# Decay attention with two gated layers on one core: weights converted by 32-bit passes, states summed on TensorE, idle products taken out, orders made anew

## Chip, core and metric

One core of a Trainium2 chip runs the whole program in one launch. The metric is the device time of an execution in microseconds. The kernel before took 938.72 us, the median of three runs (938.11 to 939.4).

## What is computed

An attention with a decaying state, then two dense layers with gates, in float32 and with float64 weights that come as they are (q, k, v, alpha: 4 batches, 8 heads, 768 positions, 48 columns; weights 384 x 2048 and 2048 x 384 for each layer):

```python
for t in range(S):
    state = alpha[:, :, t, :, None] * state + np.einsum('bhd,bhe->bhde', k[:, :, t], v[:, :, t])
    y[:, :, t] = np.einsum('bhd,bhde->bhe', q[:, :, t], state)
x = y as rows of 384 columns                  # 3072 rows
h = x @ w_in;  x = (h * np.tanh(softplus(h))) @ w_out     # first layer
h = x @ w_in2; return (h * np.cos(h)) @ w_out2            # second layer
```

## The kernel before

**Attention in pieces.** The positions are cut into 12 steps `u` of 64; each step has two pieces `(u, hb)`, 24 in all, each for half of the batches and all heads. A piece loads alpha, k, q and v, takes two running products along the positions on DVE (`scan`, L316, and `scan2`, L334), scales k and q by them (`keys`, L338, and `queries`, L348, on DVE or POOL by the sets `KPOOL` and `QPOOL`), transposes k on PE (`turn`, L366), multiplies keys and queries (`scores`, L380 and L381), masks them out of PSUM (`causal`, L388 to L391) and multiplies by v and by the state at once (`out_mm`, L401 to L405): rows of the left tiles `VE`, `VO` (`three`) hold v and the state, rows of the right tiles `RE`, `RO` the scores and the queries. Both pieces of a step share one pair `RE0`, `RO0`.

**States.** After a piece's output, `state_mm` (L465) makes the step's own product, `state_add` (L477) adds it to the state in `VE` and `VO` by four DVE instructions that read PSUM (L475: four copies on ACT in the first step), and `state_mul` (L485) scales it by the step's decay by two instructions on POOL or, for the numbers in `MULS`, on DVE. The next step's output needs it.

**Weights.** For each of 16 slices of a layer, `load_w` (L220) brings 768 float64 columns as pairs of 32-bit words, and six passes make a float32 of each, split into a rounded part `wh` and a rest `wl`: `conv_x` takes bits of the low word or of 16 bits of the high one (L230, L232 or L235), `conv_s` the sign (L241 or L244), `conv_b` scales (L251 or L253), `conv_c` merges (L257), `conv_d` rounds (L261 or L263) and `conv_e` subtracts (L267). Strings and sets at the head (`TOPS`, `SIGNS`, `SCALES`, `ROUNDS`, `LOWS`) choose engine and form: `v` with a 16-bit result on DVE, `b` a 32-bit shift on DVE, `a` ACT, `p` POOL and so on. The raw words of the second layer use the two `three` tiles in turn.

**Layers.** A step of 512 rows and one slice is `mm1` (nine products, L528 to L530), the gate on ACT and DVE, a split of the gate's result (`act_c`, L567 or L569, and `pool_c`, L574, on DVE or POOL) and `mm2` (nine products into three sums, L589 to L591). The first six slices of the first block are done in halves of 256 rows, two slices at a time. There are 192 `mm1` and 192 `mm2`.

**Order.** `Plan` takes all these pieces with an engine, an assumed cost, a due time and what they wait for, and plays them through: on each engine the piece that is ready and due first goes next. What comes out is written down in that order, and the engines follow it with semaphores. Due times come from the numbers at the head (`START`, `EARLY`, `CONV` and so on). Up to 40 idle products (`idle`, L517, 112x128 of a constant) fill PE's wait until the first `mm2`; 28 are issued. `last_heads` (L410), `fill` (L416), `y_hi` (L424) and `y_lo` (L430) hand the first four steps' outputs to the first layer.

Of the kernel before, what the change touches and what calls it, by code (L numbers as in the profile page):

```python
# [25 lines left out]
P = 128  # L26
# [10 lines left out]
START = [1448.3, 429.36, -76.954, 70.35, -175.51, -140.25, 526.61, -216.63, -872.8, 815.57]  # L37
ATT = 92.272
T0 = 526.27
HALVES = {(0, 0): 6}  # L40
SHARED = {(0, 0): 8, (0, 4): 9, (1, 0): 10}
EARLY = [-310.76, -66.363, -294.04, -73.698, 257.15, 404.09, 543.88, 902.74]
BASE = [-469.62, -69.328, 128.04, 9.9207]
BESIDE = [0, 2, 8, 7]
LAG = 0.27
LOAD_K = -68.961
LOAD_Q = -195.56
LOAD_V = 275.37
LOAD_W = 205.5
LATE = -166.65  # L50
SPLIT = [-29.4, 68.92]
CONV = [-1263, -1320.3, 881.42, 1950, -719.73, -157.26, -760.27, -551.95, -520.44, -19.586, -1457.4, -895.42, 142.68, 1400, 785.88, 1646.4, -310.36, -245.74, -228.26, -324.75, 1573, -1266, -775.74, 735.74, -740.32, 1124.8, -569.28, -195.03, -1333.7, -55.12, -2911.9, -506.3]
ELEM = 226.61
SECOND = -472.6
EVAC = -278.38
FILLED = 162.76
AHEAD = (0, 0, 0, 0, 0, 14, 6, 5, 27, 12, 27, 8, 24, 8, 12, 19)
FILL = 4
QPOOL = {*range(0, 2), *range(3, 9), 12, *range(15, 18), 20, *range(22, 24)}
MULS = {*range(7, 9), *range(10, 13), 14, *range(16, 19), 21}  # L60
LOWS = {*((0, fc) for fc in (2, 3, 10, 14, 15,)), *((1, fc) for fc in (1, 6, 10, 11, 13, 15,))}
GLS = {*range(0, 3), 5, *range(7, 9), 10, 12, *range(16, 18), *range(19, 21), 23, *range(26, 29), *range(30, 33), 34, *range(38, 40), 43, *range(45, 47), 48, *range(50, 54), *range(55, 57), *range(61, 63), *range(64, 66), 69, 71, 73, *range(76, 82), *range(86, 88), *range(89, 91), *range(92, 95), *range(97, 99), *range(100, 105), *range(108, 112), 113, *range(115, 117), *range(119, 122), 126, 129, 132, 134, 136, *range(138, 142), 145, 155, *range(157, 159), 161, 163, 167, 170, 174, 178, 180, *range(184, 186), *range(187, 189), *range(190, 192), *range(193, 199)}
IDLE = 40
KPOOL = {0, 2, 5, 7, *range(9, 11), *range(12, 18), 23}
# [3 lines left out]
ROUNDS = {*((0, fc) for fc in (0, 3, 6, 8, 9, 10, 11, 12, 13, 14,)), *((1, fc) for fc in (0, 2, 3, 4, 5, 7, 10, 11, 14, 15,))}  # L68
# [3 lines left out]
CASTS = {0, *range(2, 4), 7, *range(10, 13), *range(18, 21), *range(22, 25), 26, *range(28, 31), *range(32, 35), 36, 38, *range(42, 45), *range(47, 49), 50, 52, *range(54, 56), 57, 59, 62, 69, 73, *range(86, 88), *range(90, 92), 93, 96, 98, 102, 105, 108, *range(110, 113), *range(116, 120), 121, *range(123, 125), *range(126, 132), 133, *range(135, 137), *range(138, 140), *range(141, 143), 148, *range(150, 153), *range(154, 157), 161, *range(163, 165), 168, *range(172, 174), 175, *range(179, 181), 182, *range(185, 189), 190, *range(192, 194), 195, 197, 199}  # L72
# [9 lines left out]
class Plan:  # L82


    def __init__(self, bufs):
        self.bufs, self.pieces, self.names = bufs, [], {}
# [6 lines left out]
    def order(self):  # L93
        n = len(self.pieces)
        waits, users = [0] * n, [[] for _ in range(n)]
        holds, taken = {}, {}
        for i, (name, _, _, _, _, after, takes, drops) in enumerate(self.pieces):
            for a in after:
                if a in self.names:
                    waits[i] += 1  # L100
                    users[self.names[a]].append(i)
# [4 lines left out]
        events, out = [], []  # L106

# [12 lines left out]
        while len(out) < n:  # L120
            for e, q in ready.items():
                if free[e] > now:
                    continue
                for j, (_, i) in enumerate(q):
                    name, _, cost, _, run, _, takes, _ = self.pieces[i]
                    if may_take(takes):
                        del q[j]
                        for tag, tile_ in takes:
                            taken.setdefault(tag, []).append(tile_)
                        cost, lag = cost(now) if callable(cost) else (cost, LAG)  # L130
                        free[e] = now + cost
                        heapq.heappush(events, (now + cost, -1, i))
                        heapq.heappush(events, (now + cost + lag, 1, i))
                        out.append(run)
                        break
            if len(out) == n:
                break
# [5 lines left out]
            for tile_ in self.pieces[i][7]:  # L143
# [5 lines left out]
            for u in users[i]:  # L149
# [7 lines left out]
def chunked_path(ctx: ExitStack, tc: tile.TileContext, q, k, alpha, v1, ve, vo, w1, w2, const, out):  # L157
# [16 lines left out]
    seg_start = sb.tile([112, W65], F32, name="seg_start")  # L174
    nc.vector.memset(seg_start, 0.0)
# [164 lines left out]
    def queries(s, eng):  # L340
# [5 lines left out]
        if s not in R_:  # L346
            R_[s] = RE0, RO0
# [685 lines left out]
```

## Time and profile before

| | |
|---|---|
| median of three runs | 938.72 us |
| profiled execution, its own time | 937.42 us |
| span of the profiled execution | 935.6 us |
| PE busy | 910.2 us, 97% |
| VectorE (DVE), ScalarE (ACT), GpSimd (POOL) busy | 618.1, 668.1, 341.6 us |
| mean granted TensorE clock | 0.987 |

The span goes from the first to the last instruction. A float32 attention product counts as two instructions on PE. PE's busy time takes in the latency of overlapping products, so the count of products in a stretch says more about its pace than the share. On DVE and POOL, an instruction's duration holds what it waited for inside the engine.

### The profile page before, as it was taken

The numbers are of one execution on the slowest core, as the hardware profiler recorded it, in microseconds if no ns is written. First come the engines' busy times: TensorE is split into PE (matmuls) and PEld (weight loads), VectorE is DVE, ScalarE is ACT, GpSimd is POOL, SyncE is SP. The second block draws the span as 40 slices with busy tenths as digits, with TensorE's granted clock in tenths as the row PEclk, the third lists the DMA queues.
The fourth block names the chain that finished last, engine by engine and source line by source line (L and its number), as shares of the span: only waits on it lengthen the run. The fifth ranks groups of instructions, "written<-read, shape, count | busy, mean of one in ns | idle before, by whom it ended". The sixth has DMA issues, their size and how long they took to land.

```text
span 935.6 us, 15419 instructions
## 1 busy us (share of the span) xinstructions
PE 910.2 (97%) x6046; PEld 743.6 (79%) x6046; DVE 618.1 (66%) x876; ACT 668.1 (71%) x1030; POOL 341.6 (37%) x242
## 2 busy tenths in 40 slices
PE   8889999999999999999998999999999999999997
PEld 6678877788887787788887778888888888888886
DVE  7998999947756858733498889874545434444442
ACT  3569798989878888799998855756645555554553
POOL 4666437132235213432248443323413134122211
PEclk9689999999999999999999999999999999999999
DMA  8554334113113213120023013200000000000000
GB/s 235 168 175 129 135 121 136 55 35 96 58 59 88 83 35 104 51 73 1 1 102 101 1 68 115 89 1 1 34 35 1 0 34 1 35 1 0 35 1 36
DMA packets 25181, 59.08 MB, mean 63 GB/s; under 512 B 3856, under 2 KB 7568, under 8 KB 25104
## 3 DMA queue, kind: packets, MB, share of 16 engines
q1 hardware_dynamic: 25104, 58.05, 19.2%
q8 instruction: 48, 0.79, 0.3%
q14 instruction: 29, 0.24, 0.1%
HBM read 52.53 MB, written 4.72 MB: 61 GB/s over the span
## 4 chain that ended last, share of the span: by engine, by line
PE 84%; DVE 4%; ACT 4%; POOL 3%; issue 2%; DMA 1%; POOLq 0%; DVEq 0%; ACTq 0%
PE acc L589 13%; PE h L528 13%; PE acc L591 13%; PE acc L590 13%; PE h L530 13%; PE h L529 12%; PE sc L380 2%; PE y L404 2%; POOL wl L267 1%; PE acc L517 1%; PE pt L366 1%; PE dS L465 1%; POOL three L244 1%; DMA at<-in_alpha_chunks_dram 1%; DVE ta L544 1%
## 5 line engine op out<-in xcount | busy, mean ns | idle before, releaser
L574 POOL TENSOR_TENSOR gl<-ta,gh 128x512 fp32r<-128x512 f32 x97 | 144.6, 1491 | 359.5 <-ACT gh L569 182.0
L528 PE MATMUL h<-xhi,wh 128*128 128x512 f32 (+1 forms) x594 | 233.3, 393 | 6.5 <-DVE ta L544 4.8
L589 PE MATMUL acc<-gh,wh 128*128 128x512 f32 (+1 forms) x594 | 231.2, 389 | 0.0
L530 PE MATMUL h<-xhi,wl 128*128 128x512 f32 (+1 forms) x594 | 229.0, 385 | 1.6 <-POOL wl L267 1.6
L529 PE MATMUL h<-xlo,wh 128*128 128x512 f32 (+1 forms) x594 | 228.8, 385 | 0.0
L591 PE MATMUL acc<-gl,wh 128*128 128x512 f32 (+1 forms) x594 | 227.7, 383 | 0.1
L590 PE MATMUL acc<-gh,wl 128*128 128x512 f32 (+1 forms) x594 | 227.6, 383 | 0.0
L528 PEld LDWEIGHTS h<-xhi,wh 128*128 128x128 f32 x594 | 112.8, 190 | 32.5 <-DVE ta L544 7.3
L530 PEld LDWEIGHTS h<-xhi,wl 128*128 128x128 f32 x594 | 112.8, 190 | 24.6 <-POOL wl L267 2.3
L589 PEld LDWEIGHTS acc<-gh,wh 128*128 128x128 f32 x594 | 111.6, 188 | 23.3 <-issue 0.4
L591 PEld LDWEIGHTS acc<-gl,wh 128*128 128x128 f32 x594 | 111.6, 188 | 22.5 <-POOL gl L574 0.5
L529 PEld LDWEIGHTS h<-xlo,wh 128*128 128x128 f32 x594 | 113.0, 190 | 20.7
L590 PEld LDWEIGHTS acc<-gh,wl 128*128 128x128 f32 x594 | 111.7, 188 | 21.0
L556 DVE SCALAR_TENSOR_TENSOR tb<-tb,ta 128x512 f32<-128x512 f32 x96 | 72.4, 755 | 58.2 <-ACT tb L553 58.1
L559 ACT ACTIVATE tb<-tb 128x512 f32<-128x512 f32 x96 | 60.6, 631 | 60.3 <-DVE tb L556 60.1
L549 ACT ACTIVATE ta<-h 128x512 f32<-128x512 f32 x96 | 57.4, 598 | 61.3 <-POOL gl L574 31.3
L562 DVE TENSOR_TENSOR ta<-h,tb 128x512 f32<-128x512 f32 x96 | 66.1, 689 | 49.8 <-ACT tb L559 49.7
L544 DVE TENSOR_TENSOR ta<-h,ta 128x512 f32<-128x512 f32 x96 | 64.3, 684 | 48.8 <-ACT ta L541 48.3
L567 DVE CAST gh<-ta 128x512 fp32r<-128x512 f32 x101 | 59.7, 594 | 55.4 <-PE acc L590 54.6
L574 DVE TENSOR_TENSOR gl<-ta,gh 128x512 fp32r<-128x512 f32 x95 | 78.3, 827 | 27.2 <-ACT gh L569 26.4
L536 ACT ACTIVATE ta<-h 128x512 f32<-128x512 f32 x96 | 57.4, 598 | 42.5 <-PE h L530 37.9
L569 ACT CAST gh<-ta 128x512 fp32r<-128x512 f32 x91 | 56.2, 619 | 37.8 <-PE acc L590 31.6
(136 smaller groups left out, 1300.8 us busy)
## 6 DMA issues: line engine op xcount, KB each, us to landing
wr<-in_w_dram SPq DMA_DIRECT2D x16, 768.0 KB, 4.8
three<-in_w_dram SPq DMA_DIRECT2D x16, 768.0 KB, 4.2
at<-in_alpha_chunks_dram SPq DMA_DIRECT2D x23, 227.9 KB, 2.8
kt<-in_k_chunks_dram SPq DMA_DIRECT2D x23, 224.0 KB, 2.6
qt<-in_q_chunks_dram SPq DMA_DIRECT2D x23, 224.0 KB, 3.3
vt<-in_v_chunks_dram SPq DMA_DIRECT2D x21, 192.0 KB, 2.6
out_dram<-o SPq DMA_DIRECT2D x15, 256.0 KB, 2.1
three<-in_ve_chunks_dram SPq DMA_DIRECT2D x24, 128.0 KB, 2.5
```

The source lines that it names most:

```text
L528: nc.tensor.matmul(h, hi[:, f], xh, start=kc == 0, stop=False)
L529: nc.tensor.matmul(h, hi[:, f], xl, start=False, stop=False)
L530: nc.tensor.matmul(h, lo[:, f], xh, start=False, stop=kc == 2)
L544: nc.vector.tensor_tensor(ta_[i], h_.pop(i), ta_[i], op=ALU.mult)
L556: nc.vector.scalar_tensor_tensor(out=tb_[i], in0=tb_[i], scalar=MAGIC, in1=ta_[i], op0=ALU.subtract, op1=ALU.subtract)
L559: nc.scalar.activation(tb_[i], tb_[i], AF.Sin, scale=-TWO_PI)
L562: nc.vector.tensor_tensor(ta_[i], h_.pop(i), tb_.pop(i), op=ALU.mult)
L567: nc.vector.tensor_copy(gh_[i], ta_[i])
L574: eng.tensor_tensor(gl_[i], ta_.pop(i), gh_[i].bitcast(F32)[:, :], op=ALU.subtract)
L589: nc.tensor.matmul(acc[d][:, c0:c1], hi[:, f], gh, start=first, stop=False, skip_group_check=True)
L590: nc.tensor.matmul(acc[d][:, c0:c1], lo[:, f], gh, start=False, stop=False, skip_group_check=True)
L591: nc.tensor.matmul(acc[d][:, c0:c1], hi[:, f], gl, start=False, stop=last, skip_group_check=True)
```

## The change

- **Weights**: `conv_x` on DVE is always the 32-bit shift, on POOL always 16 bits to 32; `conv_s` is always a bitwise instruction of two inputs on DVE; `conv_d` may be on POOL; which engine does what is chosen anew.
- **States**: in the first four steps, the scaling reads the state out of PSUM, on DVE, by four instructions; in steps 1 to 3 (six pieces) PE adds the old state to the product, by four products with the unit matrix. `state_add` stays for the later steps.
- **Queries**: the second piece of a step takes two `tb` tiles for `RE` and `RO`, which the second layer uses later.
- **Idle products**: none is issued.
- **Plan**: attention products that are due within 6 us are put beside each other; DVE is taken to wait for the end of a POOL instruction, and POOL for that of a DVE one; all numbers are new.

```diff
-IDLE = 40
-TOPS = "aavvaavvavavvvvv", "abwvpqbvwapqabwv"
-SIGNS = "vvvvvvvvvvvvvvvv", "pvovpovvopvopvov"
-SCALES = "vaaavaaaavaavava", "aavaapaavaapaava"
+SUMS = 4
+JOIN = 6.0
+IDLE = 0
+TOPS = "apvapppvavpvapav", "vvpvpapavapvappp"
+SCALES = "aaaavaaaavavvpap", "pavvvvpvppappapa"
+ROUNDS = "aapapapppapvavvp", "ppappvpvpvaavvap"
...
     def conv_x(la, fc):
-        if how == "b":
+        if how == "v":
             nc.vector.tensor_scalar(low, low, 29, None, op0=ALU.logical_shift_right)
...
         else:
-            eng = nc.gpsimd if how in "pq" else nc.vector
-            eng.tensor_scalar(low if how in "qw" else w16[:, :, 0], w16[:, :, 1], 2.0**-13, 2.0**-14 - 0.5, op0=ALU.mult, op1=ALU.add)
+            nc.gpsimd.tensor_scalar(low, w16[:, :, 1], 2.0**-13, 2.0**-14 - 0.5, op0=ALU.mult, op1=ALU.add)
     def conv_s(la, fc):
-        if SIGNS[la][fc] == "o":
-            nc.vector.scalar_tensor_tensor(out=low, in0=high, scalar=0x80000000, in1=low, op0=ALU.bitwise_and, op1=ALU.bitwise_or)
-        else:
-            eng = nc.vector if SIGNS[la][fc] == "v" else nc.gpsimd
-            eng.tensor_scalar(halves(la, fc)[:, :, 1], high.bitcast(F32), 0.0, 32768.0, op0=ALU.is_lt, op1=ALU.mult)
+        nc.vector.scalar_tensor_tensor(out=low, in0=high, scalar=0x80000000, in1=low, op0=ALU.bitwise_and, op1=ALU.bitwise_or)
...
     def conv_d(la, fc):
+            nc.gpsimd.tensor_scalar(wh[la, fc], low, 1.0, 1.0, op0=ALU.mult, op1=ALU.mult)
...
         if s not in R_:
-            R_[s] = RE0, RO0
+            R_[s] = [stile([P, N], F32, "tb", "R").rearrange("p (g c) -> p g c", c=C) for _ in range(2)] if s[1] else (RE0, RO0)
...
     def state_mm(s):
+        more = 0 < s[0] < SUMS
+        for bb in range(2 * more):
+            for V, lo in ((VE[s[1]], 0), (VO[s[1]], 64)):
+                r = slice(lo, lo + 48)
+                nc.tensor.matmul(dS[bb][r], ident[:, r], V[0:112, bb::2, 0:48], start=True, stop=False, skip_group_check=True)
...
     def state_mul(s):
+        if s[0] < SUMS:
+            dS = dS_.pop(s)
+            for bb in range(2):
+                for V, lo in ((VE[s[1]], 0), (VO[s[1]], 64)):
+                    r = slice(lo, lo + 48)
+                    nc.vector.tensor_tensor(V[r, bb::2, 0:48], dS[bb][r], aend[r, pos[s], bb::2].to_broadcast([48, 4, 48]), op=ALU.mult)
             return
...
+            for u in users[i] if kind else near[i]:
...
+    def dve(alone):
+        def cost(now):
+            took = max(plan.free[POOL] - now - 0.14, 0.0) + alone
+            plan.held[0] = now + took
+            return took, LAG
+        return cost
```

Three places in the order. The first is DVE around the first states. Before, up to the first four adds, which belong to step 1 (`dS_494`, `dS_495` are its two products in PSUM, `three_73` a state's tile):

```order
L338 TENSOR_TENSOR kt<-kt,at 112x512
L244 TENSOR_SCALAR wr<-wr 128x768
L257 SCALAR_TENSOR_TENSOR wr<-wr 128x768 x2
L390 TENSOR_TENSOR spare<-sc,cst 64x512
L391 TENSOR_TENSOR spare<-sc,cst 64x512
L261 CAST wh<-wr 128x768
L430 TENSOR_TENSOR xlo<-y,xhi 128x3x128
L267 TENSOR_TENSOR wl<-wr,wh 128x768
L316 SCALAR_TENSOR_TENSOR Pt<-at,seg_start 112x520
L267 TENSOR_TENSOR wl<-wr,wh 128x768
L477 TENSOR_TENSOR three_73<-three_73,dS_494 48x4x48 x2
L477 TENSOR_TENSOR three_73<-three_73,dS_495 48x4x48 x2
```

Now, where the scaling of step 0 stands (L505), with the sign (L257) and the merge (L270) of the first slice around it:

```order
L350 SCALAR_TENSOR_TENSOR at<-at,rend 112x520
L257 SCALAR_TENSOR_TENSOR wr<-wr 128x768
L505 TENSOR_TENSOR three_73<-dS_189,aend 48x4x48 x2
L505 TENSOR_TENSOR three_73<-dS_190,aend 48x4x48 x2
L364 TENSOR_TENSOR three_73<-qt,Pt 112x512
L446 TENSOR_TENSOR xlo<-y,xhi 128x3x128
L270 SCALAR_TENSOR_TENSOR wr<-wr 128x768
L404 TENSOR_TENSOR aux<-sc,cst 128x512
```

The four adds have become four scalings, which now stand in step 0 too, and the next queries follow them on DVE.

The second is POOL at the same place. Before, with the scalings of step 0 on it (L485):

```order
L338 TENSOR_TENSOR kt<-kt,at 112x512
L267 TENSOR_TENSOR wl<-wr,wh 128x768
L485 TENSOR_TENSOR three_73<-three_73,aend 48x8x48 x2
L485 TENSOR_TENSOR three_74<-three_74,aend 48x8x48 x2
L329 COPY aend<-Pt 112x8
L348 TENSOR_TENSOR spare<-qt,Pt 112x512
L267 TENSOR_TENSOR wl<-wr,wh 128x768
```

Now, with the truncation (L252) and the rounding (L279) of slices of the weights:

```order
L354 TENSOR_TENSOR kt<-kt,at 112x512
L252 TENSOR_SCALAR wr<-wr 128x768
L283 TENSOR_TENSOR wl<-wr,wh 128x768
L345 COPY aend<-Pt 112x8
L283 TENSOR_TENSOR wl<-wr,wh 128x768
L345 COPY aend<-Pt 112x8
L279 TENSOR_SCALAR wh<-wr 128x768
L252 TENSOR_SCALAR wr<-wr 128x768
```

The scalings and the queries are gone from POOL here, and passes over the weights stand in their place.

The third is SP, which issues the transfers. Before:

```order
L286 DMA at<-in_alpha_chunks_dram 112x521
L291 DMA kt<-in_k_chunks_dram 112x512
L296 DMA qt<-in_q_chunks_dram 112x512
L286 DMA big<-in_alpha_chunks_dram 112x521
L299 DMA three_73<-in_ve_chunks_dram 64x512
L300 DMA three_73<-in_vo_chunks_dram 64x512
L838 DMA cst<-in_const_dram 128x272
```

Now:

```order
L307 DMA kt<-in_k_chunks_dram 112x512
L315 DMA three_73<-in_ve_chunks_dram 64x512
L316 DMA three_73<-in_vo_chunks_dram 64x512
L302 DMA at<-in_alpha_chunks_dram 112x521
L326 DMA vt<-in_v_chunks_dram 128x384
L312 DMA qt<-in_q_chunks_dram 112x512
```

The first alpha has moved from the first place to the fourth, behind a piece's keys and values.

## Rows read from the trace of the kernel before

**Rows 1.** The page: busy time by engine, share of the span, instructions.
```profile
PE 910.2 (97%) x6046; PEld 743.6 (79%) x6046; DVE 618.1 (66%) x876; ACT 668.1 (71%) x1030; POOL 341.6 (37%) x242
```

**Rows 2.** Windows: stretch, length, busy us (x) of PE, PEld, DVE, ACT, POOL; clock; DMA.
```profile
20.00:40.00 20.00, 15.26 (x226) 12.23 (x226) 19.55 (x21) 10.86 (x23) 14.69 (x9) 0.67 0.68 212
480.00:570.00 90.00, 84.73 (x369) 68.48 (x368) 77.35 (x86) 70.94 (x103) 54.34 (x29) 1.00 0.20 71
600.00:700.00 100.00, 100.00 (x443) 82.81 (x442) 59.20 (x87) 58.98 (x102) 29.03 (x20) 1.00 0.07 25
```

**Rows 3.** The chain that ended last: start us, us, what; its seam and end.
```profile
81.77 0.32 PE acc L589
...
930.41 0.24 PE acc L591
930.68 0.59 ACT o L614
```

**Rows 4.** Waits of PE: us in total, times, longest.
```profile
PE h L528 <- DVE ta L544: 4.8, 4, 2.3
PE h L528 <- DVE ta L562: 1.4, 1, 1.4
```

**Rows 5.** Durations by line, ns: min/median/max; passes over weights.
```profile
L257 DVE SCALAR_TENSOR_TENSOR wr<-wr x16: 933/948/2332, 20.1 to 174.8; 128x768 uint32<-128x768 uint32 x16
L244 DVE TENSOR_SCALAR wr<-wr x16: 985/1028/3292, 18.2 to 173.3; 128x768 uint16<-128x768 f32 x16
L235 DVE TENSOR_SCALAR wr<-wr x10: 1025/1124/2453, 26.8 to 170.7; 128x768 uint16<-128x768 uint16 x10
L230 DVE TENSOR_SCALAR three<-three x3: 554/1741/2236, 461.0 to 592.1; 128x768 uint32<-128x768 uint32 x3
```

**Rows 6.** Timeline, DVE and POOL: start us, us, instruction; two pairs beside each other.
```profile
33.93 1.85 POOL L267 TENSOR_TENSOR wl<-wr,wh 128x768 fp32r<-128x768 f32 x1
34.21 2.45 DVE L235 TENSOR_SCALAR wr<-wr 128x768 uint16<-128x768 uint16 x1
...
55.16 1.88 POOL L267 TENSOR_TENSOR wl<-wr,wh 128x768 fp32r<-128x768 f32 x1 [6.97 <-issue]
55.61 2.24 DVE L257 SCALAR_TENSOR_TENSOR wr<-wr 128x768 uint32<-128x768 uint32 x1
```

**Rows 7.** Durations by line, as in rows 5; the states.
```profile
L477 DVE TENSOR_TENSOR three<-three,dS x80: 319/357/384, 45.1 to 380.2; 48x192 f32<-48x192 f32 x80
L485 POOL TENSOR_TENSOR three<-three,aend x24: 824/1034/3595, 25.5 to 371.2; 48x384 f32<-48x384 f32 x24
```

**Rows 8.** Durations by line, as in rows 5; queries, and POOL's scaling.
```profile
L348 POOL TENSOR_TENSOR three<-qt,Pt x13: 1178/1212/1813, 5.9 to 398.1; 112x512 f32<-112x512 f32 x13
L348 DVE TENSOR_TENSOR three<-qt,Pt x9: 636/673/1035, 22.4 to 366.4; 112x512 f32<-112x512 f32 x9
L251 POOL TENSOR_SCALAR three<-three x2: 889/1226/1562, 504.5 to 568.5; 128x768 f32<-128x768 f32 x2
```

**Rows 9.** Windows as in rows 2, then of PE alone: clock, `mm1` halves, scores.
```profile
27.00:44.00 17.00, 15.78 (x139) 13.09 (x140) 16.60 (x19) 7.25 (x13) 8.50 (x7) 0.50 0.50 155
44.00:61.00 17.00, 14.70 (x211) 12.28 (x211) 15.63 (x21) 12.68 (x19) 7.87 (x6) 1.00 0.62 208
...
40.63:44.48 3.85, 3.85 (x21) 0.56 0.12 38
46.27:48.51 2.24, 2.24 (x21) 1.00 0.99 337
53.77:54.85 1.08, 1.08 (x34) 1.00 0.98 398
```

**Rows 10.** The chain around a state's product: start us, us, what.
```profile
230.27 0.51 PE dS L465 x32
230.77 0.43 PE h L528
```

**Rows 11.** The chain in the second layer: a sign pass on POOL.
```profile
492.81 4.00 POOL three L244
```

More of the change, by code (lines that the diff above doesn't have):

```diff
@@ L43 @@
[L43 to L55, printed above, removed]
@@ L82, with __init__ @@
 class Plan:
-    def __init__(self, bufs):
-        self.bufs, self.pieces, self.names = bufs, [], {}
+    def __init__(self, bufs, quick):
+        self.bufs, self.quick, self.pieces, self.names = bufs, quick, [], {}
+        self.group, self.joined = ("turn", "scores", "out_mm", "fill", "state_mm"), False
     def add(self, name, engine, cost, due, run, after=(), takes=(), drops=()):
@@ L94, in order @@
         n = len(self.pieces)
-        waits, users = [0] * n, [[] for _ in range(n)]
+        waits, users, near = [0] * n, [[] for _ in range(n)], [[] for _ in range(n)]
         holds, taken = {}, {}
@@ L100, in order @@
                     waits[i] += 1
-                    users[self.names[a]].append(i)
+                    j = self.names[a]
+                    same = self.pieces[i][1] == self.pieces[j][1] and self.pieces[i][1] in self.quick
+                    (near if same else users)[j].append(i)
             for tile_ in drops:
@@ L121, in order @@
             for e, q in ready.items():
-                if free[e] > now:
+                if free[e] > now or (e == "pool" and held[0] > now):
                     continue
[L124 to L134, printed above, removed]
-                        break
+                pick, limit = None, 0.0
+                for j, (due, i) in enumerate(q):
+                    if pick is not None and due > limit:
+                        break
+                    name, takes = self.pieces[i][0], self.pieces[i][6]
+                    if (pick is None or name[0] in self.group) and may_take(takes):
+                        first, pick = pick is None, j
+                        if not first or e != "pe" or not self.joined or name[0] in self.group:
+                            break
+                        limit = due + JOIN
+                if pick is None:
+                    continue
+                _, i = q.pop(pick)
+                name, _, cost, _, run, _, takes, _ = self.pieces[i]
+                for tag, tile_ in takes:
+                    taken.setdefault(tag, []).append(tile_)
+                cost, lag = cost(now) if callable(cost) else (cost, LAG)
+                if e == "pe":
+                    self.joined = name[0] in self.group
+                free[e] = now + cost
+                heapq.heappush(events, (now + cost, -1, i))
+                heapq.heappush(events, (now + cost + min(lag, NEAR), 0, i))
+                heapq.heappush(events, (now + cost + lag, 1, i))
+                out.append(run)
             if len(out) == n:
@@ L142, in order @@
                 continue
-            for tile_ in self.pieces[i][7]:
+            for tile_ in self.pieces[i][7] if kind else ():
                 holds[tile_] -= 1
@@ L464, in state_mm @@
                     e0 = 96 * p + (lo // 64) * 48
-                    nc.tensor.matmul(dS[bb][lo : lo + 48, p, :], kT[r, p, lo : lo + 48], vt[r, e0 : e0 + 48], start=True, stop=True, skip_group_check=True)
+                    nc.tensor.matmul(dS[bb][lo : lo + 48, p, :], kT[r, p, lo : lo + 48], vt[r, e0 : e0 + 48], start=not more, stop=True, skip_group_check=True)
     def state_add(s):
@@ L624, in chunked_path, with pe @@
     ticks, begun = {}, []
-    def pe(us, rows=1.0):
+    def pe(us, rows=1.0, enter=0.0):
         def cost(now):
-            t, left = now, us
+            t, left = now, us + (0.0 if plan.joined else enter)
             while left > 1e-6:
@@ L643, in begin, with pool @@
         return first_sums
-    def dve(alone, beside):
-        return lambda now: (beside if plan.free[POOL] > now + 0.3 * alone else alone, LAG)
-    def pool(alone, beside):
-        return lambda now: (beside if plan.free[DVE] > now + 0.3 * alone else alone, LAG)
+    def dve(alone):
[4 more added lines that the diff above has]
+        return cost
+    def pool(alone):
+        return lambda now: (alone - 0.2 * (now == plan.held[0]), LAG)
     def dma(kib):
@@ L802, in chunked_path @@
+        add(("inv_end", s), DVE, 0.14, d + 1.0, f(inv_end, s), [("scan", s), ("scan2", r)])
         add(("guard", s), ACT, 0.85, d + 1, f(guard, s), [("ld_a", s)], [], [])
-        add(("keep_end", s), POOL, pool(0.2, 0.6), d + 1, f(keep_end, s), [("scan", s)], [], [("Pt", n)])
-        add(("scan2", s), DVE, dve(1.25, 1.65), d + 1.7, f(scan2, s), [("guard", s), ("inv_end", s)], [], [])
+        add(("keep_end", s), POOL, pool(0.22), d + 1, f(keep_end, s), [("scan", s)], [], [("Pt", n)])
+        add(("scan2", s), DVE, dve(1.18), d + 1.7, f(scan2, s), [("guard", s), ("inv_end", s)], [], [])
```

132 lines of the change are left out of this document (74 added, 58 removed).

## The prediction

> **What bounds the kernel now.** I read the page first: PE is busy 97% of the span [rows 1]. That average hides two kinds of time, so I read the windows next. From 600 to 700 us PE issues 443 products without a gap, 0.226 us each, so a half step of nine (`mm1` or `mm2`) takes 2.03 us; nothing but fewer products could shorten such a stretch. From 20 to 40 us it is different: PE counts 15.3 us of 20 as busy at a granted clock of 0.67, and VectorE 19.6 of 20 [rows 2]. The start is set by the vector engines, the rest by PE, with a few stalls between.
>
> The seam between the two is found in the chain: from about 81.8 us, when the group of the second `mm2` starts, nearly every piece of the chain is a product, up to the last one at 930.65 us; then come one evacuation, the output's transfer and the end at 935.64 [rows 3]. So the time is made of the seam's time T, 848.9 us of PE from there, and a tail of 5.0 us. Within the 848.9 the waits view names stalls before `mm1` on DVE's gate products, 4.8 and 1.4 us [rows 4]. Most of them lie in one stretch, with the refilling of the array behind each: from 480 to 570 us there are 369 products, where 399 would fit at the later pace, so 30 x 0.226 = 6.8 us are lost [rows 2]. The prediction is therefore a new T, a new PE total behind it, and new stalls.
>
> **How DVE and POOL share the start.** DVE instructions in flight beside a POOL instruction do not run beside it. L257 takes 0.93 us alone, but 2.24 us when it starts while POOL's L267 runs from 55.16 to 57.04: it ends 0.8 us after POOL does. L235 does the same at 34.21, 2.45 us for 1.03 [rows 5, 6]. Instructions that read PSUM are exempt: the 80 adds on L477 lie between 319 and 384 ns, with POOL busy beside many of them [rows 7]. So for the start I add DVE and POOL together. With the shortest duration of each kind, less the 0.08 us by which a row may start before its predecessor's end, all that stands in the two engines' order ahead of the second `mm2` sums to 59.3 us on DVE and 30.6 on POOL, 89.9 for a T of 81.8: 8 us more than the time, which is the part of the PSUM readers that did lie beside POOL. I scale by 81.8/89.9.
>
> **The change, part by part, up to the seam.**
> - *States.* Ahead of the seam stand five states. Gone are three groups of four adds on DVE (12 x 0.357 = 4.3 us) and five scalings on POOL, two instructions each (0.82 at least, 1.03 in the median; I take 0.93, so 9.3) [rows 7]. New are five groups of four scalings on DVE that read the sum in PSUM, 48x192, the same shape as the adds: 20 x 0.357 = 7.1. Net -6.4, and POOL's 9.3 us of holding others up are gone.
> - *Keys and queries.* Five of them go from POOL (1.18) to DVE (0.64) [rows 8]: -2.8. Odd queries have their own two buffers now, so they don't wait for the product of the piece before; that adds no instruction.
> - *Weights.* Four 16-bit truncations on DVE (L235, 1.1) become two 32-bit shifts there (L230, 0.55) and four on POOL; four roundings move to POOL, three of them from DVE (0.55, as the shift); one more low part (L267, 1.86) and one more merge (0.93) fall ahead of the seam, one low part leaves DVE. The sign pass goes from L244 (0.99 at least) to the form of L257 (0.93) [rows 5, 6]. The POOL passes have no row of their own; the nearest are POOL's scalings of the same 768 columns at 0.89 us and the subtraction of L267 at 1.86, and I take 0.95, nearest to the scaling since both have one input [rows 8]. Sum of this item: +4.0, up to +11 at the upper end.
> - *The rest* (two small conversions of gate values earlier): +1.0.
>
> The sum is 6.4 + 2.8 - 4.0 - 1.0 = 4.2 us less, and T falls by 4.2 x 81.8/89.9 = 3.8 to 78.0. The ends: if only instructions that hold POOL up count, 73.8 becomes 66.6 and T falls by 7.2, to 74.6; if DVE's own order is all that counts, 59.3 becomes 59.2 and T stays 81.8. The first transfers move too: keys and values go ahead of the first alpha, so the first scan starts later; but the twelve idle products that stood ahead of the first transpose on PE are gone. I cost the two at nothing together, since one makes the first scores late and the other early.
>
> The rule of the Trainium skill that speaks against this ("SBUF — State Buffer", section "Who interferes with whom") is that a DVE instruction with at most one SBUF input outside the two-port modes does not contend with GpSimd, while one with two SBUF inputs does. By it the old 16-bit passes would have run beside POOL and the new two-input sign pass would not; the trace disagrees, L235 waited in [rows 6].
>
> **The clock.** PE ran at 0.50 from 27 to 44 us and at 1.00 from 44 to 61, where nine idle products lay among the real ones [rows 9]. Two `mm1` halves took 3.85 us mostly at 0.50, and 2.24 at 1.00 [rows 9]. Without the idle products some of that fast stretch is lost. It costs nothing while DVE and POOL are later than PE, which they are there; a group of products that DVE waits for (scores take 1.08 us at 1.00 [rows 9]) is longer by the same ratio, 0.7 to 0.8 us. I take one of these on the path, 0.7, with the ends 0 and 10 (below). T = 78.7.
>
> **Behind the seam.** One fill (0.8) moves behind it. Three of the six new state sums fall there. Their products, two pairs of 192 columns, have no row; scores, 8 pairs of 64 columns, take 1.08 [rows 9], so a sum is 4 x 192/(16 x 64) of that, 0.8 us; a state's own 32 products, 0.51 [rows 10], and twice 0.8, if pairs don't overlap, are the ends. Three: +2.4 (1.5 to 4.8). Leaving an attention group costs the next product 0.43 instead of 0.23 us [rows 2, 10]; the order has 64 such visits for 69, since six outputs now stand beside the next scores: -1.0. Stalls: the chain at the longest one passes through a sign pass on POOL, 4.00 us from 492.81 [rows 11], which is one of four in that layer. The change leaves no sign pass on POOL; the conversions of the second layer sum to 76 us on both engines instead of 86. But they still stand in the same stretch with two buffers, so I leave 2 of the 6.8 us, with the ends 0 and 9.
>
> PE ends at 78.7 + 848.9 + 0.8 + 2.4 - 1.0 - 6.8 + 2.0 = 925.0; with the tail of 5.0 the span is 930.0, for 935.6. The profiled execution took 937.4, 1.8 more than its span, and the median of the runs, 938.7, is 1.3 above that: 933.1.
>
> **Rivals.**
> - *The clock decides (slower).* Without the idle products PE stays at 0.50 from 45 us to the seam. The products that ran in the fast stretch, three `mm1`/`mm2` pairs (1.6 us more each), scores, outputs, transposes, fill and state (some 3 more together), and three sums at low clock (0.8 more each) add 10 us; PE then is later than DVE, and T is 88: 942 us. It decides if the clock is at half for over some 15 us between 45 and 75. For it: without idle products the rows there are sparse. Against: the rise to 1.00 at 44 us came behind the first `mm1` halves [rows 9], and these stay. Chance 0.14.
> - *The skill's rule holds.* The old 16-bit passes (7.6 + 4.2 us) don't count among those that hold POOL up; the sum is 62.0 before and 66.6 now, T 86.0: 940.4, no change at best. Against it stand [rows 6]. Chance 0.05.
> - *Stalls return.* The new passes on POOL meet the gates' low parts in the second layer and 8 us of stalls stand there: 939, no change. Chance 0.13.
> - *POOL was the whole matter.* T is 74.6 and no stall is left: 927. Chance 0.20.
>
> **How the numbers follow.** The forecast has the other 0.48, and runs from 928 to 937 by itself. The range takes in the larger gain and half of the slower cases, with the unknown POOL and sum prices: 923 to 942. A measurement here can tell 0.2%, 1.9 us, from no change, so the borders are 936.8 and 940.6. Faster: 0.20, nearly all of the forecast (0.45) and a part of the returned stalls (0.05): 0.70. Same: 0.14. Slower: 0.16.
>
> **What would show it.** Right: the second `mm2` at 76 to 81 us; no POOL instruction on the states of the first four steps; adds in PSUM of 0.8 us; no wait of `mm1` for a gate over 1 us between 480 and 570. Wrong: a granted clock of 0.50 in most of 45 to 75 us with DVE idle behind PE; POOL's roundings over 1.5 us; PE waiting on weights' low parts after 480 us.

## The result and the profile after

The changed kernel takes 928.62 us, the median of four runs (926.98 to 930.75); the kernel before, beside it, 938.41 (937.38 to 939.40, four runs). The ratio is 0.9897, with an interval of 0.9873 to 0.9921: faster, by 9.8 us where 5.6 were predicted. The profiled execution took 928.11 us, its span is 926.3; the views of each kernel below are of one execution.

The page's busy times, which answer to [rows 1]:

```profile
PE 897.1 (97%) x6038; PEld 737.3 (80%) x6038; DVE 609.9 (66%) x889; ACT 656.1 (71%) x1010; POOL 292.1 (32%) x233
```

POOL lost 49.5 us of work and PE 13.1; DVE and ACT 8 and 12. The seam in PE's timeline (start us, us, instruction):

```profile
78.77 0.38 PE L614 MATMUL acc<-gh,wh 128*128 128x256 f32 x1
```

The end in the chain, as in [rows 3]:

```profile
920.90 0.24 PE acc L616
921.14 0.02 issue
921.16 0.59 ACT o L639
```

On PE's timeline of the kernel before, the second `mm2` starts here (81.77 in the chain of [rows 3], which counts from the end of what stands ahead):

```profile
81.70 0.39 PE L589 MATMUL acc<-gh,wh 128*128 128x256 f32 x1
```

It starts 2.9 us sooner now, and PE needs 842.4 us from there, 6.5 less than the 848.9 of before. So two thirds of the gain lie behind the seam. The windows (columns as in [rows 2]) say where; the first line is of the kernel before, the others are of the change:

```profile
80.00:160.00 80.00, 77.22 (x764) 62.86 (x765) 76.58 (x106) 71.06 (x105) 43.80 (x29) 1.00 0.40 129
80.00:160.00 80.00, 79.48 (x721) 64.31 (x722) 69.91 (x102) 71.38 (x101) 27.80 (x21) 1.00 0.38 123
480.00:570.00 90.00, 89.80 (x397) 74.03 (x396) 80.89 (x104) 71.36 (x105) 36.93 (x28) 1.00 0.25 88
570.00:700.00 130.00, 130.00 (x575) 107.45 (x574) 75.11 (x105) 75.87 (x129) 46.35 (x33) 1.00 0.07 25
```

From 480 to 570 us PE issues 397 products, where it issued 369 [rows 2]: 28 more of 0.226 us, 6.3 us. POOL is busy for 36.9 us there instead of 54.3. Ahead of 160 us PE's pauses behind the seam are 0.5 us, and were 1.9. PE's waits, as in [rows 4]:

```profile
PE sc L396 <- DVE kt L354: 11.6, 2, 10.6
PE pt L382 <- DVE three L505: 6.0, 2, 3.4
PE y L432 <- ACT st L426: 3.6, 2, 2.8
PE h L553 <- DVE ta L569: 1.3, 3, 0.6
```

Of the waits before `mm1` on DVE's gate products 1.3 us are left, of 6.2. The largest wait is that of the first scores for the first keys. The second line is new: a transpose waits for the PSUM slot that a state holds until DVE has scaled it. PE's timeline shows one of these, behind the new sum:

```profile
56.46 0.86 PE L479 MATMUL dS<-three,cst 112*48 112x192 f32 x8
57.25 0.57 PE L486 MATMUL dS<-vt,kT 64*48 64x48 f32 x32
60.47 0.57 PE L382 MATMUL pt<-cst,kt 112*128 112x112 f32 x4 [2.64 <-DVE three L505]
```

A sum takes 0.79 us, from 56.46 to 57.25; the estimate was 0.8. The clock from 45 to 75 us, where the prediction's rival put a half, was granted at 0.89, with DVE busy for 27.7 of 30 us:

```profile
45.00:75.00 30.00, 24.59 (x330) 21.75 (x331) 27.66 (x40) 19.84 (x31) 17.21 (x13) 0.89 0.56 185
```

### The profile page after: what moved, and what is told of

It is laid out like the page before. It is cut to its first block, busy times and chain, and to the rows that moved or that the text cites. A ratio compares the mean times of both kernels' runs of the same rounds, so it can differ in the third digit from the quotient of the medians.

```text
span 926.3 us, 15375 instructions
## 1 busy us (share of the span) xinstructions
PE 897.1 (97%) x6038; PEld 737.3 (80%) x6038; DVE 609.9 (66%) x889; ACT 656.1 (71%) x1010; POOL 292.1 (32%) x233
## 4 chain that ended last, share of the span: by engine, by line
PE 89%; DVE 5%; ACT 2%; DMA 1%; issue 1%; POOL 1%; SPq 0%; POOLq 0%; DVEq 0%; ACTq 0%
PE h L553 14%; PE acc L614 14%; PE acc L616 13%; PE acc L615 13%; PE h L554 13%; PE h L555 13%; PE sc L396 2%; PE y L420 2%; PE dS L486 1%; PE pt L382 1%; DMA wr<-in_w_dram 1%; DVE wr L257 1%; DVE three L505 1%; DVE wr L270 1%; DVE Pt L332 1%
## 5 line engine op out<-in xcount | busy, mean ns | idle before, releaser
L599 POOL TENSOR_TENSOR gl<-ta,gh 128x512 fp32r<-128x512 f32 x91 | 128.2, 1410 | 361.5 <-ACT gh L594 180.2
L581 DVE SCALAR_TENSOR_TENSOR tb<-tb,ta 128x512 f32<-128x512 f32 x96 | 80.2, 836 | 81.8 <-ACT tb L578 81.7
L569 DVE TENSOR_TENSOR ta<-h,ta 128x512 f32<-128x512 f32 x96 | 63.8, 683 | 54.6 <-ACT ta L566 54.3
L599 DVE TENSOR_TENSOR gl<-ta,gh 128x512 fp32r<-128x512 f32 x101 | 74.4, 741 | 21.9 <-ACT gh L594 18.7
L592 DVE CAST gh<-ta 128x512 fp32r<-128x512 f32 x102 | 51.2, 504 | 49.7 <-PE acc L615 49.2
```

Source lines behind the costliest of these rows:

```text
L569: nc.vector.tensor_tensor(ta_[i], h_.pop(i), ta_[i], op=ALU.mult)
L581: nc.vector.scalar_tensor_tensor(out=tb_[i], in0=tb_[i], scalar=MAGIC, in1=ta_[i], op0=ALU.subtract, op1=ALU.subtract)
L599: eng.tensor_tensor(gl_[i], ta_.pop(i), gh_[i].bitcast(F32)[:, :], op=ALU.subtract)
```

## Experiments

"The theory" in the texts on record is that of the prediction: DVE and POOL bind the start, and POOL's sign passes made the stalls from 480 us. Each kernel keeps the order of the kernel it is made from, except where planning is named. Medians are set against 928.6 us for the changed kernel and 937.0 to 939.0 for the one before, which ran again beside each kernel; the ratios are to that.

### Sign passes

The change with four sign passes put back on POOL (e3):

```diff
     def conv_s(la, fc):
...
+        if la and fc in (0, 4, 9, 12):
+            nc.gpsimd.tensor_scalar(halves(la, fc)[:, :, 1], high.bitcast(F32), 0.0, 32768.0, op0=ALU.is_lt, op1=ALU.mult)
+            return
```

> The changed kernel, its order kept, with four of the second layer's sign passes (slices 0, 4, 9 and 12) back on POOL. Theory (sign passes of about 4 us on POOL made the stalls of 480 to 570 us): products on PE in 480 to 570 fall from 397 to 375 to 390 and the time rises by 3 to 7 us, to 932 to 936. Rival (the new order and split of the other passes made the stalls go): 393 or more products there, the time within 1.5 of 928.6.

Measured: 938.72 us, ratio to before 1.0004 (0.9990 to 1.0019). Four instructions give back the whole gain. The windows of this run:

```profile
480.00:570.00 90.00, 86.86 (x375) 71.06 (x374) 74.30 (x95) 67.72 (x101) 43.09 (x29) 0.98 0.25 88
570.00:700.00 130.00, 126.46 (x557) 104.06 (x556) 77.00 (x104) 73.85 (x127) 50.77 (x34) 1.00 0.07 25
```

And PE's waits before `mm1`:

```profile
PE h L556 <- DVE ta L572: 5.5, 4, 3.1
PE h L556 <- DVE ta L590: 3.5, 2, 2.0
```

22 products are missing in the first stretch, as expected, and 18 more in the second: 9.0 us. A wait of 1.3 us at 458 us makes up most of the rest of the loss, since PE needs 852.8 us from the second `mm2`, 10.5 more than in the change. The time lies above the 932 to 936 expected: the passes stand from 453 to 569 us, and I had costed one stretch alone. How one such pass reaches PE is seen in the timelines of POOL, DVE and PE (start us, us, instruction, idle time before it and its releaser):

```profile
486.52 3.93 POOL L258 TENSOR_SCALAR three<-three 128x768 uint16<-128x768 f32 x1
...
490.49 0.96 DVE L273 SCALAR_TENSOR_TENSOR three<-three 128x768 uint32<-128x768 uint32 x1 [3.61 <-POOL three L258]
...
493.09 1.61 POOL L602 TENSOR_TENSOR gl<-ta,gh 128x512 fp32r<-128x512 f32 x1 [0.43 <-DVE gh L595]
493.46 2.05 DVE L260 SCALAR_TENSOR_TENSOR three<-three 128x768 uint32<-128x768 uint32 x1
494.65 2.00 POOL L224 TENSOR_TENSOR xlo<-x,xhi 128x512 fp32r<-128x512 f32 x1
495.54 1.93 DVE L273 SCALAR_TENSOR_TENSOR three<-three 128x768 uint32<-128x768 uint32 x1
...
498.73 1.27 DVE L572 TENSOR_TENSOR ta<-h,ta 128x512 f32<-128x512 f32 x2
...
499.47 0.50 PE L556 MATMUL h<-xhi,wh 128*128 128x512 f32 x1 [3.11 <-DVE ta L572]
```

The merge on DVE waits 3.6 us for the sign pass. DVE's later passes meet two subtractions on POOL (L602, L224) and take 2 us each instead of 1, the gate's product behind them comes late, and PE waits 3.1 us for the PSUM slot that it frees, until nine microseconds after the pass that began it had ended.

The same from the other side, the kernel before with those four passes on DVE (e4; slice 4's pass ahead, `conv_x`, goes from `p` to `q`, the form that writes all 32 bits):

```diff
-TOPS = "aavvaavvavavvvvv", "abwvpqbvwapqabwv"
+TOPS = "aavvaavvavavvvvv", "abwvqqbvwapqabwv"
...
-        if SIGNS[la][fc] == "o":
+        if SIGNS[la][fc] in "op":
             nc.vector.scalar_tensor_tensor(out=low, in0=high, scalar=0x80000000, in1=low, op0=ALU.bitwise_and, op1=ALU.bitwise_or)
```

> The kernel before, its order kept, with the four sign passes of the second layer that ran on POOL (slices 0, 4, 9 and 12) done on DVE in the 32-bit form that five others of that layer have there already (for slice 4 the pass ahead writes all 32 bits). Theory (a sign pass of 4 us on POOL holds DVE up, and DVE then PE): products on PE in 480 to 570 us rise from 369 to 385 to 397, the time falls by 4 to 8 us from 938.5, to 930.5 to 934.5. Rival (it takes the new order as well): under 378 products, the time 937 to 940.

Measured: 932.02 us, 0.9932 (0.9915 to 0.9949), 6.9 us less. Its window:

```profile
480.00:570.00 90.00, 89.35 (x393) 73.28 (x392) 80.76 (x96) 73.68 (x107) 45.73 (x27) 1.00 0.20 71
```

24 of the 28 products are back without any other part of the change. From the second `mm2` PE needs 843.3 us, 5.6 less than before, where the whole change needs 6.5 less; of the rest, 0.8 us is the start, sooner in this execution, which no sign pass of the second layer, the first at 457 us, can move. What follows: this one part, which is four instructions moved, is worth 6.9 of the 9.8 us in the old order (4.8 to 8.0 by the interval), and all of it in the new one.

### States

The change with the states of steps 0 to 3 as before: in `state_mm` no sums, then copies or adds, then scalings on POOL (e2).

```diff
-        more = 0 < s[0] < SUMS
+        more = False
...
-                    nc.vector.tensor_tensor(V[r, bb::2, 0:48], dS[bb][r], aend[r, pos[s], bb::2].to_broadcast([48, 4, 48]), op=ALU.mult)
+                    if s[0] == 0:
+                        nc.scalar.copy(V[r, bb::2, 0:48], dS[bb][r])
+                    else:
+                        nc.vector.tensor_tensor(V[r, bb::2, 0:48], V[r, bb::2, 0:48], dS[bb][r], op=ALU.add)
+            for V, lo in ((VE[s[1]], 0), (VO[s[1]], 64)):
+                r = slice(lo, lo + 48)
+                nc.gpsimd.tensor_tensor(V[r, :, 0:48], V[r, :, 0:48], aend[r, pos[s]].to_broadcast([48, NSEG, 48]), op=ALU.mult)
```

> The changed kernel, its order kept, with the states of steps 0 to 3 as before: an ACT copy in step 0, else four adds on DVE, then two scalings on POOL; the six sums on PE are gone. Theory: the start is longer by the states' share of the port sum (6.4 us x 0.91 = 5.8, second mm2 at 84 to 85), three sums of 0.8 us behind it go: 928.6 + 5.8 - 2.4 = 932, between 929 and 935. Rival (POOL's scalings lie beside DVE's PSUM readers and cost the start nothing): second mm2 within 1 us of 78.8, the time 926 to 927.

Measured: 944.43 us, 15.8 over the change, and slower than the kernel before: 1.0065 (1.0040 to 1.0091). The second `mm2` starts at 86.46, 7.7 later, and PE needs 850.7 us from there, 8.4 more, with three sums fewer; from there to 160 us it pauses for 6.7 us, where the change has 0.5. Its waits name POOL:

```profile
PE h L561 <- POOL wl L283: 5.2, 2, 2.8
PE h L559 <- DVE ta L575: 3.4, 2, 3.2
PE acc L622 <- POOL gl L605: 3.2, 1, 3.2
```

Neither expectation covers it; so the next kernel has the scalings on DVE (e11; its edit against e2):

```diff
-                nc.gpsimd.tensor_tensor(V[r, :, 0:48], V[r, :, 0:48], aend[r, pos[s]].to_broadcast([48, NSEG, 48]), op=ALU.mult)
+                nc.vector.tensor_tensor(V[r, :, 0:48], V[r, :, 0:48], aend[r, pos[s]].to_broadcast([48, NSEG, 48]), op=ALU.mult)
```

> As e2_states_undone (copies or adds, then scalings, no sums on PE), but the two scalings of a state on DVE, not on POOL. Theory (what cost 15.8 us there are the scalings on POOL, which stand in front of POOL's weight passes and hold DVE up): of the 15.8 at least 8 go, the time is 930 to 936, the second mm2 at 79 to 83. Rival (the adds and copies, or the order that was made without them, cost it): the time is 939 or more, the second mm2 at 85 or later.

Measured: 937.44 us, 0.9979 (0.9966 to 0.9992); second `mm2` at 84.52, 847.3 us from there. Seven of the 15.8 us were POOL's scalings, 3.4 of them behind the seam and 1.9 ahead of it in the profiled executions, and the waits on POOL's `wl` and `gl` are gone with them; the wait on DVE's `ta` is up to 4.9 us. The scalings on DVE:

```profile
L511 DVE TENSOR_TENSOR three<-three,aend x16: 550/556/2137, 19.2 to 124.5; 48x384 f32<-48x384 f32 x16
```

It falls between the two expectations: the other 8.8 us are DVE's work, or the order, which was made without it. To tell these apart, the same with a new plan, which knows the adds and scalings (e14; the due times at the head are still those of the change):

```diff
-SUMS = 4
+SUMS = 0
```

> The changed kernel with the sums of states on PE switched off and the order planned anew for it: four adds on DVE per state, then scalings, on POOL for pieces 0, 1, 2, 4 and 6, on DVE for 3, 5 and 7; the planner's due times stay those of the change. Theory (what e2 showed is mostly the states' work on DVE and POOL, 5.8 us by the port sum, plus an order that was not made for it): the second mm2 at 82 to 86, the time 932 to 938, below e2's 944. Rival (the states cost all of the 15.8 whatever the order): 941 or more. Second rival (a planned order hides them): within 2 of 928.6.

Measured: 948.72 us, 1.0114 (1.0096 to 1.0133). The planned order is the worst of the three: from 40 to 100 us PE is busy for 40.7 of 60, at a granted clock of 0.70, and DVE for 52.4. All of the loss is ahead of the seam, which comes at 101.5; from there PE needs 840.1 us. By the numbers the rival's 941 or more came out, but nothing here separates the states' own cost from due times that were found for another set of instructions. It stays open. What the runs do show: a part has no single price. The sign passes cost 10.1 us undone in the new order and gave 6.9 in the old one, and the states, undone with the order kept, cost 8.8 or 15.8; 10.1 and 8.8 are together more than the 9.8 by which the two kernels differ.

### The clock

The kernel before, in which `idle` returns without issuing anything (e5):

```diff
         if not acc_:
-            w = ps.tile([P, N], F32, tag="acc0", name="acc0")
+            return
```

> The kernel before, its order kept, without its idle products. Theory (the clock decides nothing at the start, DVE and POOL do): the second mm2 starts within 1 us of 81.8 and the time is within 1.5 us of 938.5. Rival (the idle products kept the clock up and that was worth something there): the second mm2 at 84 to 87, the time 940.5 to 944.

Measured: 938.26 us, 0.9998 (0.9988 to 1.0009); second `mm2` at 81.63. The granted clock from 44 to 61 us fell from 1.00 [rows 9] to 0.78, the products of the first `mm2` at 55 us took 0.41 us each for 0.28, and it cost nothing. In the kernel before, the rival is out.

The other way round, 28 idle products put into the change, of 512 columns where the kernel before had 128, `heat` of them ahead of each piece named (e1):

```diff
+        heat = {("scores", 0, 0): 12, ("fill", 0, 1): 6, ("scores", 1, 1): 3, ("turn", 1, 1): 7}
...
+                for _ in range(heat.get((name, *run.args[0]), 0)):
+                    idle()
```

> The changed kernel, its order kept, with 28 idle products of 512 columns put back on PE: 12 ahead of the first scores, 6 ahead of the second fill, 3 ahead of the scores of the fourth piece, 7 ahead of that piece's transpose; all in places where PE waits. Theory (DVE and POOL decide the start, the clock nothing): the first two mm1 halves, 2.08 and 1.65 us in the changed kernel, come out nearer 1.2, but the second mm2 still starts at 78.8 plus or minus 1 and the time stays within 927 to 930. Rival (the lost idle products cost time at the start): the second mm2 starts at 74 to 77 and the time is 924 to 926.5.

Measured: 930.61 us, 0.9924 (0.9899 to 0.9949); second `mm2` at 80.89. PE's timeline shows what they cost:

```profile
2.08 9.86 PE L542 MATMUL acc<-seg_start 112*112 112x512 f32 x12 [2.08 <-DVE seg_start L194]
...
27.45 4.90 PE L542 MATMUL acc<-seg_start 112*112 112x512 f32 x6
```

They take 0.8 us each there, so that the first twelve end 1.3 us after the first scores could have started, and the next six stand in front of a fill. Too many in the wrong places; so a third kernel (e13) has eight, in the two waits of a transpose alone (the second four write the PSUM tile of the next `mm1`):

```diff
...
+                if run.args[0] == (1, 1):
+                    for _ in range(4):
+                        idle()
+                if run.args[0] == (2, 0):
+                    h_[2] = ps.tile([P, N], F32, tag="h", bufs=3, name="h")
+                    for _ in range(4):
+                        nc.tensor.matmul(h_[2][0:112], seg_start[:, 0:112], seg_start[:, 0:N], start=True, stop=True, skip_group_check=True)
```

> The changed kernel, its order kept, with 8 idle products of 512 columns on PE, 4 in each of the two waits of a transpose for its PSUM slot (43.2 to 46.6 and 57.8 to 60.5 us). Theory (the two mm1 behind these waits run at a low clock, 3.6 and 3.4 us for 2.3, and lie on the path): they take 2.3 to 2.8, the second mm2 starts 1 to 2.2 us sooner, the time is 926 to 927.8. Rival (DVE and weights decide the start, the clock nothing): the second mm2 at 78.4 to 79.5, the time 928 to 930.

Measured: 929.43 us, 0.9907 (0.9887 to 0.9928). The `mm1` behind the first wait ran at a granted 1.00, two halves of 1.17 us, the one behind the second still took 3.5; the second `mm2` started at 77.73, 1.0 sooner, in the profiled execution, and the median is no better. The rival's 928 to 930 holds for the time. The seam, in the fastest of the four executions, lies at the near edge of the theory's 1 to 2.2 us sooner; it is within what one start differs from the next by (below), so that a gain of about 1 us is neither shown nor excluded.

A slow clock in plain sight is found in the next kernel, made for another end: three state scalings moved in the order to right behind their products, to shorten the transposes' new wait (e9).

```diff
...
+    for s in ((1, 0), (1, 1), (2, 0)):
+        mul = next(r for r in ordered if name(r) == "state_mul" and r.args[0] == s)
+        ordered.remove(mul)
+        ordered.insert(1 + next(j for j, r in enumerate(ordered) if name(r) == "state_mm" and r.args[0] == s), mul)
```

> The changed kernel with three state scalings on DVE (pieces (1, 0), (1, 1) and (2, 0)) moved in the order to right behind the products that make them; two scans, a pass over 32 bits and a product of queries now stand behind them, not ahead. Theory (the transposes' new wait for the PSUM slot, 3.4 and 2.6 us, sets the end of the start): both waits fall under 1.5 us, the second mm2 starts at 76 to 77.5, the time is 925.5 to 927.5. Rival (the scans and keys behind them are then what is late): second mm2 at 78 or later, the time 928 or more.

Measured: 936.31 us, 0.9977 (0.9963 to 0.9992), 7.7 over the change. The waits fell to 0.9 us each, as meant, and the second `mm2` starts at 86.39. The timelines of POOL and PE have the wait that takes their place:

```profile
62.53 3.56 POOL L283 TENSOR_TENSOR wl<-wr,wh 128x768 fp32r<-128x768 f32 x1
66.14 0.58 PE L555 MATMUL h<-xhi,wl 128*128 128x256 f32 x1 [3.63 <-POOL wl L283]
```

And the window around it:

```profile
60.00:82.00 22.00, 15.54 (x141) 13.51 (x138) 17.66 (x25) 14.37 (x20) 10.59 (x7) 0.69 0.31 95
```

A weight pass that the scaling pushed back by 1.3 us came to meet other DVE instructions, so that POOL's low part took 3.6 us instead of 1.9 and PE waited 3.6 for it. Behind that wait the clock stood at half: the next `mm1` halves took 2.08 and 2.05 us, at 71.3 and 73.3, where they take 1.17 in the change. That is at least 1.8 us of the 7.6 that the seam is late by; how the rest divides between this wait and those on the gate is not shown. So the rival's mechanism exists. In the change, too, a half of `mm1` behind each of the two waits runs at half pace, 2.1 us; e13, which took that from the first, won at most the 1.0 us above.

### What sets the start

The chain of the change runs on DVE, and for 4.3 us on POOL, from 35.4 to 61.1 us; behind that it is mostly PE, from 62.8 to 66.2 us and from 72.8 to the seam. Two passes over weights on it (start us, us, what):

```profile
47.20 1.61 DVE wr L264
52.45 1.30 POOL wh L279
```

Four passes over weights moved to ACT, out of the change: two from DVE, two from POOL, the two above among them (e8).

```diff
-        w16, low, how = halves(la, fc), wr[la, fc][:, :, 0], TOPS[la][fc]
+        w16, low, how = halves(la, fc), wr[la, fc][:, :, 0], "a" if (la, fc) == (0, 2) else TOPS[la][fc]
...
-        if SCALES[la][fc] != "a":
+        if SCALES[la][fc] != "a" and (la, fc) != (0, 4):
...
-        elif ROUNDS[la][fc] == "a":
+        elif ROUNDS[la][fc] == "a" or (la, fc) in ((0, 2), (0, 4)):
```

> The changed kernel, its order kept, with four weight passes of the start moved to ACT, which idles there: the lower-half pass of slice 2 and the scaling of slice 4 from DVE (0.55 and 1.61 us), the roundings of slices 2 and 4 from POOL (1.29 each, which hold DVE up). Theory (DVE and POOL decide the start): the second mm2 starts 2 to 3.5 us sooner, at 75.3 to 76.8, the time is 925 to 927. Rival (weight transfers, ACT or PE decide it): second mm2 at 78.5 or later, the time 928 or more.

Measured: 929.04 us, 0.9915 (0.9892 to 0.9938); second `mm2` at 79.13. This is the rival's outcome. DVE's busy time from 40 to 60 us fell from 18.0 to 15.4 us, and the seam did not move. DVE now waits for ACT, whose copy of the outputs comes 1.4 us later behind the passes it was given:

```profile
55.47 0.56 DVE L446 TENSOR_TENSOR xlo<-y,xhi 128x384 fp32r<-128x384 f32 x1 [3.31 <-ACT xhi L440]
```

Only the two passes of slice 2, which lie where ACT idles (e12):

```diff
-        w16, low, how = halves(la, fc), wr[la, fc][:, :, 0], TOPS[la][fc]
+        w16, low, how = halves(la, fc), wr[la, fc][:, :, 0], "a" if (la, fc) == (0, 2) else TOPS[la][fc]
...
-        elif ROUNDS[la][fc] == "a":
+        elif ROUNDS[la][fc] == "a" or (la, fc) == (0, 2):
```

> As e8_start_to_act, but slice 2's two passes alone: its lower-half pass from DVE and its rounding from POOL to ACT, which idles there (37.9 to 41.9 us) and has no weight pass ahead of the output's copies after 50. Theory (in e8 the two passes of slice 4 made ACT late, and that ate the gain): the second mm2 at 77 to 78.3, the time 926.5 to 928.5. Rival (DVE's order gains nothing, the start waits for something else): the second mm2 at 78.5 or later, 928 or more.

Measured: 930.34 us, 0.9904 (0.9880 to 0.9928); second `mm2` at 81.48. No gain either, the rival's outcome again. Last, the transfers (e10):

```diff
...
+    a, b = order[:2]
+    first = [("ld_a", a), ("ld_k", a), ("ld_q", a), ("ld_a", b), ("ld_v", a)]
+    first = [next(r for r in ordered if name(r) == w and r.args[0] == s) for w, s in first]
+    ordered = first + [r for r in ordered if r not in first]
```

> The changed kernel with the first transfers in the order alpha, keys, queries, the second alpha, values, and the rest as it was; nothing else moves. Theory (what I cost at nothing: the later first scan is hidden behind the weights' transfers): the first scores start some 2.5 us sooner, at 8 to 8.5, but the second mm2 within 0.7 of 78.8 and the time 928 to 930. Rival (the late first scan sits on the path): the second mm2 at 76 to 77.5, the time 925.5 to 927.5.

Measured: 928.78 us, 0.9896 (0.9876 to 0.9915). The first scores start at 7.99 for 10.56, the second `mm2` at 79.70: hidden, as costed. What hides them is not the weights: the transpose behind these scores waits 3.6 us for the constants' transfer, where it waited 0.5, and starts at 13.61 for 13.08.

None of the kernels tried beats the change by more than the runs scatter.

One thing the runs say together. In the change and in the six kernels that alter only its start and keep its sums (idle products, passes, transfers, scalings), PE needs 842.3 to 842.4 us from the second `mm2` to its last product, while the second `mm2` starts anywhere from 77.7 to 86.4. And the kernel with sign passes on POOL, which is the change itself up to 450 us, has it at 77.39 where the change has 78.77. One start thus differs from the next by 1.4 us at least, and what the change's four runs differ by (3.8 us) most likely lies there, since the rest takes the same time in seven executions.

## Why the prediction was right, and where it was off

- **The seam, 78.7 us**: 78.77. That it agrees to 0.1 us is luck, where one start differs from the next by 1.4; its reason is only half shown. The port sum says that whatever leaves DVE or POOL ahead of the seam shortens it. With the states it has the sign, and not the sizes: undone with the scalings on POOL, priced at 5.8 us (6.4 x 0.91), they move the seam by 7.7; with the scalings on DVE the same sum would give 2.4 us, an estimate (ten scalings of 0.55 and twelve adds for twenty scalings of 0.357, times 0.91), and it moves by 5.8. Both are in an order not made for them. With the weights it doesn't agree: four passes taken off the two engines, two of them from the chain, moved nothing, since ACT, to which they went, then came late. The start hops between the vector engines, ACT and PE, and a sum over two of them is not what it waits for.
- **States: "POOL's 9.3 us of holding others up are gone"**: that the scalings on POOL hold others up is shown. With them back there, 7.0 us more are lost than with them on DVE. But the prediction put all of it ahead of the seam, where 1.9 us of it are seen, little more than a start scatters by.
- **The clock, 0.7 us, and its rival at 942**: in the kernel before, the idle products were worth nothing, within 0.12%, and in the change the clock was granted at 0.89 where the rival has a half. The seam has too much scatter to see the 0.7.
- **Transfers and the first twelve idle products, nothing together**: nothing speaks against it. The transfers, tried alone, gave nothing. The twelve were not tried by themselves: all 28 taken out of the kernel before gave nothing either.
- **A fill, 0.8, and three sums, 2.4**: 0.78 and 3 x 0.79.
- **64 visits for 69, -1.0**: behind the seam PE returns from attention to the layers 58 times, for 62 before, four fewer and not five; not tried by itself. Moving scores away from the outputs would have moved DVE's order too.
- **Stalls, "I leave 2 of the 6.8 us"**: the step that failed, in its size. By the same count 0.45 us are left (397 products, where 399 would fit). I left 2 because the passes over weights still stand in that stretch; but most of the stall came from the sign passes, and the chain [rows 11] had named one. Stalls ahead of 160 us were not in the sum at all: between the seam and there PE idled for 1.9 us before and for 0.5 now; e4 leaves them at 1.9, so it isn't the sign passes that ended these.
- **The end**: PE's last product was put at 925.0 and ends at 921.1. Of the 3.9 us the stalls are 1.6 and those ahead of 160 us 1.3; the other 1.0 lies in the products' pace, outputs and visits, each below what I can tell. The tail is 5.2 for 5.0. The median lies 0.5 above the profiled execution instead of 1.3.

Of the rivals, "POOL was the whole matter" (927) came nearest in time and is half right: no stall is left, but the seam is not at 74.6. That the stalls return was wrong. The rule of the Trainium skill ("SBUF — State Buffer", "Who interferes with whom") gave 940.4 with a seam at 86.0; 928.6 and 78.8 were measured. Applying it took the old 16-bit passes to be outside the two-port modes; their 1.03 us, where the 32-bit shift takes 0.55 [rows 5], speaks for that, but no run shows the mode. Two-input passes do wait for POOL, as the rule has it: the new sign pass takes 0.93 us alone, and 1.62 from 130.76 us in the change, where a scaling on POOL ends at 131.59.

Of the signs named, the seam, the sums and the waits of `mm1` came out as for "right". One of those for "wrong" came too: a rounding on POOL took 1.64 us, from 77.35 us, at the seam itself. The median of the first layer's is 1.29, where 0.95 was put for it.

## What to carry to other kernels

When a stretch bound by one engine stalls, follow the chain back to the longest single instruction on a slow engine and move that one first: four sign passes of 15.7 us in all were most of a change that rewrote every order. A part's price, found by undoing it in an order tuned with it, is not its share: here it was 10.1 us in one order and 6.9 in the other, so undo it in both before you divide the gain. And an engine that is 90% busy in a stretch isn't its bound by that: take work off it, see whether the end moves, and see what the engine that took the work over does.

## What the runs showed that I had not expected

The sign pass on POOL is slow by its form. A comparison from 32 bits to 16 over 768 columns takes 3.93 us, while POOL's other one-input passes over as many columns take from 0.88 us. What in the form costs the time, the comparison or the 16-bit result, is only half separated: in the kernel before, two passes on POOL with a 16-bit result and no comparison took 1.95 and 2.55 us, and two of the same with a 32-bit result 0.94 and 1.20. By lines (ns: min/median/max), first the sign pass of the experiment, then the rounding and the 16-bit pass in the change:

```profile
L258 POOL TENSOR_SCALAR three<-three x4: 3930/3932/4092, 453.3 to 569.1; 128x768 uint16<-128x768 f32 x4
```

```profile
L279 POOL TENSOR_SCALAR wh<-three x7: 876/1142/1276, 456.6 to 591.2; 128x768 fp32r<-128x768 f32 x7
L252 POOL TENSOR_SCALAR three<-three x7: 879/1197/1677, 466.4 to 581.7; 128x768 uint32<-128x768 uint16 x7
```

The granted clock of a row doesn't always tell PE's pace at the start. PE alone in three windows of the change (stretch, length, busy us, clock, DMA):

```profile
38.10:40.20 2.10, 2.10 (x12) 1.00 0.97 284
48.67:50.76 2.09, 2.09 (x11) 0.50 1.02 376
67.99:70.33 2.34, 2.34 (x23) 1.00 0.92 264
```

The first two each hold one half `mm1` of nine products (the counts take in the ends of neighbours), in the same 2.1 us, the one in a row at 1.00 and the other at 0.50; in the third two halves take 2.34. A pace is better read from the products' own times.
